# Chunk attention and a gated MLP on one core: value product made transposed, row sums by matmuls with ones, single loads of q and k, and every engine in the order of an event model

## The chip, the cores and the metric

The kernel runs on one core of a Trainium2 chip. The metric is the device time of one execution in microseconds (us), lower is better. The engines are named as the profile names them: PE is TensorE (matmuls), PEld its weight loads, DVE VectorE, ACT ScalarE, POOL GpSimd, SP SyncE, which here only issues DMA transfers (SPq is its queue). The span in a profile is one execution from its first to its last instruction. Some runs fell in a slower state (two of six of e7, one each of e10 and e13, and a few of the kernel before); the ratios leave them out, the medians do not.

## The reference

Eight batches, eight heads, 576 positions, 64 values per head; attention only inside chunks of 64 positions. Its output, as rows of 512 values, goes through a gated MLP whose gate mixes positions with a 576x576 matrix.

```python
scores = scale * np.matmul(q_c, k_c.transpose(0, 1, 2, 4, 3))   # 64x64 per chunk and head
attn = np.exp(scores - max); attn = attn / (sum(attn) + 1e-09)
x = np.matmul(attn, v_c)                                        # -> (8, 576, 512)
h = np.maximum(x @ w_in, 0.0)                                   # 512 -> 1024
u, v = h[..., :512], h[..., 512:]
v_n = (v - mean(v)) / sqrt(var(v) + 1e-06)
v_s = np.einsum('ts,bsd->btd', w_spatial, v_n) + b_spatial[None, :, None]
out = (u * v_s) @ w_out
```

The tokens are worked on as 36 tiles of 128 rows. Every fifth tile of nine lies across two batches.

## The kernel before

Per tile: load q, k and v; cast to bf16 on GpSimd; transpose q and k on TensorE (TR); scores (QK); exponential on ScalarE; value product (AV); normalise on VectorE; transpose the result x (XT), since the input products want x with its features on partitions. Then the input products HV (per tile) and U (per four tiles), the statistics, the spatial products SP (64 units of five matmuls) and the output products FIN (36). Only TensorE and GpSimd are put in a hand-made order here; the others follow it.

```python
def load(t):                                   # two transfers for each of q and k, in halves of four heads
    for name, src in (("q", q), ("k", k)):
        for r0, n, b, s in pieces(t):
            for e in (0, 1):
                nc.sync.dma_start(out=f[r0:r0 + n, e, :],
                    in_=src[b, 4 * e:4 * e + 4, s:s + n, :].rearrange("h (p r) d -> p h (r d)", r=4))
    ...
def AV(t):                                     # out: chunk rows on partitions; column 64 is the row sum
    for h in range(H):
        for c in (0, 1):
            c0 = c * 64
            nc.tensor.matmul(o[c0:c0 + 64, h, 0:65], eT[c0:c0 + 64, h // 4, (h % 4) * 64:(h % 4) * 64 + 64],
                             va[c0:c0 + 64, h, :], start=True, stop=True)
    nc.vector.reciprocal(rz, o[:, :, 64:65])
    nc.vector.tensor_tensor(x, o[:, :, 0:64], rz.to_broadcast([128, H, D]), op=ALU.mult)
def XT(t):
    for m in range(4):
        nc.tensor.transpose(ps[:, m * 128:(m + 1) * 128], x[:, 2 * m:2 * m + 2, :]..., permb)
    nc.vector.tensor_copy(xT[g][:, :, r * 128:(r + 1) * 128], ps[:, 0:512]...)
...
def try_sp():                                  # spatial products of batch b
    ...                                        # only when its statistics group (an odd batch: two) and its input products U are done
    ready = clock[0] + 12.0
```

The softmax here doesn't subtract the row's maximum and nothing guards it: scores larger than these inputs give would overflow.

Of the kernel before, what the change touches and what calls it, by code (L numbers as in the profile page):

```python
# [12 lines left out]
PSUM = bass.MemoryType.PSUM  # L13


@with_exitstack
def kernel(
# [11 lines left out]
    nc = tc.nc  # L29

    B, H, S, D = q.shape
    CH = 64
# [3 lines left out]
    NTOK = B * S  # L36
    NT = NTOK // 128
    NG = NTOK // 512
    HS = S // 2
    att_scale = 1.0 / float(D) ** 0.5  # L40
    out_flat = out.rearrange("b s d -> (b s) d")

    def pool(name, bufs, **kw):
        return ctx.enter_context(tc.tile_pool(name=name, bufs=bufs, **kw))

    consts = pool("consts", 1)
    persist = pool("persist", 1)
    xT_pool = pool("xT_pool", 4)
    uT_pool = pool("uT_pool", 6)
    att_in = pool("att_in", 4)  # L50
    att_bf = pool("att_bf", 4)
    att_sb = pool("att_sb", 3)
    relu_pool = pool("relu_pool", 12)
    vn_pool = pool("vn_pool", 20)
    tail_pool = pool("tail_pool", 3)
    stat_pool = pool("stat_pool", 3)
    bst_pool = pool("bst_pool", 4)
    gat_pool = pool("gat_pool", 3)
    osb_pool = pool("osb_pool", 4)

    ps_tr = pool("ps_tr", 1, space=PSUM)
    ps_sc = pool("ps_sc", 1, space=PSUM)
    ps_o = pool("ps_o", 1, space=PSUM)
    ps_big = pool("ps_big", 3, space=PSUM)

# [4 lines left out]

# [3 lines left out]

    permb = consts.tile([128, 128], BF16, name="permb")
    for c in (0, 1):
        nc.vector.tensor_copy(permb[:, c * 64:c * 64 + 64].rearrange("p (l r) -> p l r", r=4),
                              identb[:, c * 64:c * 64 + 64].rearrange("p (r l) -> p l r", r=4))
# [3 lines left out]
    NVB = 6  # L82
    vaug = [persist.tile([128, H, 65], BF16, name=f"vaug{i}") for i in range(NVB)]
    for i in range(NVB):
        nc.vector.memset(vaug[i][:, :, 64:65], 1.0)

    xT, uT = {}, {}


    w_in_sb = persist.tile([128, 4, d_ff], BF16, name="w_in_sb")  # L90
    w_out_sb = persist.tile([128, 4, d_model], BF16, name="w_out_sb")
    ws_nat = persist.tile([128, 5, S], BF16, name="ws_nat")

    ws_full = [[persist.tile([128, S], BF16, name=f"wsf{p}_{i}") for i in range(4)]
               for p in (0, 1)]
    ws_tail = [persist.tile([128, S], BF16, name=f"wst{p}") for p in (0, 1)]

    w_in_v = moe_w_in.rearrange("(c p) f -> p c f", p=128)

    def load_w_in(part, c0, c1):  # L100
        cols = slice(F, 2 * F) if part == "v" else slice(0, F)
        nc.gpsimd.dma_start(out=w_in_sb[:, c0:c1, cols], in_=w_in_v[:, c0:c1, cols])
# [8 lines left out]
    def load_w_out():  # L111
        nc.gpsimd.dma_start(out=w_out_sb, in_=moe_w_out.rearrange("(c p) f -> p c f", p=128))

    def ws_transpose(p, i):

        if i < 4:
            s0, n, dst = i * 128 + 64 * p, 128, ws_full[p][i]
        else:
            s0, n, dst = (512 if p == 0 else 0), 64, ws_tail[p]
        ps = ps_big.tile([128, 1024], BF16, name="big")  # L120
        for tb in range(5):
            m = 128 if tb < 4 else 64
            nc.tensor.transpose(ps[:n, tb * 128:tb * 128 + m],  # L123
                                ws_nat[:m, tb, s0:s0 + n], identb[:m, :m])
        if (i + p) % 2:
            nc.vector.tensor_copy(dst[:n, :], ps[:n, 0:S])
        else:
            nc.scalar.copy(dst[:n, :], ps[:n, 0:S])


    st = {}

    def pieces(t):

        b, s = divmod(t * 128, S)
        if s + 128 <= S:
            return [(0, 128, b, s)]
        return [(0, 64, b, s), (64, 64, b + 1, 0)]

    def load(t):  # L140
        f32 = {}

        for name, src in (("q", q), ("k", k)):
            f = att_in.tile([128, 2, 4 * D], FP32, name=f"{name}f")
            for r0, n, b, s in pieces(t):
                for e in (0, 1):
                    nc.sync.dma_start(  # L147
                        out=f[r0:r0 + n, e, :],
                        in_=src[b, 4 * e:4 * e + 4, s:s + n, :].rearrange("h (p r) d -> p h (r d)", r=4))
            f32[name] = f  # L150
        f = att_in.tile([128, H, D], FP32, name="vf")
        for r0, n, b, s in pieces(t):
            nc.sync.dma_start(out=f[r0:r0 + n], in_=v[b, :, s:s + n, :].rearrange("h s d -> s h d"))
        f32["v"] = f
        st[t] = {"f32": f32}

    def cast(t, after_each=()):
        f32 = st[t].pop("f32")

        qb = att_bf.tile([128, 4, 2, D], BF16, name="qb")  # L160
        kb = att_bf.tile([128, 4, 2, D], BF16, name="kb")
        for dst, name in ((qb, "q"), (kb, "k"), (vaug[t % NVB][:, :, 0:64], "v")):
            x = f32[name]
            nc.gpsimd.tensor_copy(dst, x if name == "v" else x.rearrange("p e (r d) -> p r e d", r=4))  # L164
            for f in after_each:
                f(name)
        st[t] = {"q": qb, "k": kb}

    def cols(c, m):

        return m * 32 + c * 16

    def TR(t):
        ps = ps_tr.tile([128, 1024], BF16, name="tr")
        for i, name in enumerate(("q", "k")):
            for r in range(4):
                c = i * 512 + r * 128
                nc.tensor.transpose(ps[:, c:c + 128],  # L178
                                    st[t][name][:, r].rearrange("p e d -> p (e d)"), permq)
        qT = att_sb.tile([128, 4, 128], BF16, name="qT")  # L180
        nc.vector.tensor_copy(qT.rearrange("p r c -> p (r c)"), ps[:, 0:512])  # L181
        kT = att_sb.tile([128, 128, 4], BF16, name="kT")
        nc.scalar.copy(kT, ps[:, 512:1024].rearrange("p (r c) -> p c r", r=4))  # L183
        st[t]["qkT"] = (qT, kT)

    def QK(t):
        qT, kT = st[t].pop("qkT")
        sc = ps_sc.tile([128, 2, 512], FP32, name="sc")
        for m in range(4):
            for c, e in ((0, 0), (1, 1), (1, 0), (0, 1)):  # L190
                p0, c0 = e * 64, c * 64
                col = cols(c, m)

                nc.tensor.matmul(sc[c0:c0 + 64, e, m * 64:m * 64 + 64],  # L194
                                 kT[p0:p0 + 64, col:col + 16, :].rearrange("p l r -> p (l r)"),
                                 qT[p0:p0 + 64, :, col:col + 16], start=True, stop=True)
        eT = att_sb.tile([128, 2, 256], BF16, name="eT")
        nc.scalar.activation(eT, sc[:, :, 0:256], AF.Exp, scale=att_scale)  # L198
        st[t]["eT"] = eT

    def AV(t):
        eT = st[t].pop("eT")
        va = vaug[t % NVB]
        o = ps_o.tile([128, H, 128], FP32, name="o")
        for h in range(H):
            for c in (0, 1):
# [320 lines left out]
```

## Time and profile before

The median of the first three runs was 226.71 us (225.56 to 228.22).

| | before |
|---|---|
| profiled span | 226.9 us, in a run timed at 228.2 us |
| PE busy | 194.7 us (86%) |
| DVE, ACT, POOL busy | 123.5, 109.5, 101.5 us |
| first spatial product | 80 us |

The busy time of PE is an upper figure, since matmuls overlap at their ends. TensorE's instructions are cut into units (a tile's transposes, its scores, one group of four matmuls, and so on). The time from one unit's start to the next one's start, at its shortest for this pair of kinds, is called **work**; all that a gap is longer than that is **idle**, a wait or a lowered clock alike, and so is the time up to the first matmul (4.7 us). Before: 183.4 us of work, 39.3 us idle, and about 4 us after the last matmul make the span of 226.9. The count has an error: in the traces of e1 to e8 and e13 to e17 the records of some 30 of the matmuls are missing, which makes a shortest step too short. e14 comes out at 182.1 where before, with the same work, has 183.4. So work can be up to 1.3 us too small there, and idle time too large by as much.

### The profile page before, as it was taken

Reading aid. Unit: us, or ns where it says so; the run is one execution under the profiler, and the core shown is the slowest. Engines: PE = TensorE matmul, PEld = TensorE weight load, DVE = VectorE, ACT = ScalarE, POOL = GpSimd, SP = SyncE. Lnnn points to the kernel's source line nnn. Section 1 sums busy time; section 2 is a strip of 40 time slices with the busy share of each in tenths; the row PEclk is TensorE's granted clock in tenths of the full one; section 3 lists DMA queues with packets and bytes.
Section 4 is the critical chain, followed back from the end, with each engine's and each line's share of the span. In section 5 each row is a group of like instructions: output and inputs, shape, how many; then the busy total and the mean of one; then the engine's idle time right before and its main releaser. Section 6 shows DMA issues by size and latency. Waiting matters only on the chain.

```text
span 226.9 us, 6144 instructions
## 1 busy us (share of the span) xinstructions
PE 194.7 (86%) x2402; PEld 120.7 (53%) x2402; DVE 123.5 (54%) x339; ACT 109.5 (48%) x202; POOL 101.5 (45%) x166
## 2 busy tenths in 40 slices
PE   1236486996795999999979999999999999999993
PEld 0123333754463586567557655576665555656551
DVE  1030533748647775578555766696565487535240
ACT  2221332774575534773544566734537774252523
POOL 3526461657935865278443192895304107040000
PEclk9999857999999999999999999999999999999999
DMA  4999999979557897955989896488822000132223
GB/s 130 188 241 221 212 198 244 242 199 243 154 155 192 226 241 215 275 167 150 235 258 293 240 304 178 123 228 223 305 92 93 2 3 1 56 150 106 107 87 147
DMA packets 65981, 40.40 MB, mean 178 GB/s; under 512 B 40800, under 2 KB 61344, under 8 KB 65952
## 3 DMA queue, kind: packets, MB, share of 16 engines
q1 hardware_dynamic: 63680, 37.76, 58.8%
q0 software_dynamic: 2272, 2.24, 6.8%
q8 instruction: 19, 0.31, 0.6%
q14 instruction: 10, 0.08, 0.1%
HBM read 32.79 MB, written 9.44 MB: 186 GB/s over the span
## 4 chain that ended last, share of the span: by engine, by line
PE 77%; DMA 9%; SPq 6%; ACT 3%; DVE 2%; issue 1%; POOL 0%; ACTq 0%; POOLq 0%
PE big L314 17%; PE big L330 14%; PE big L241 14%; PE big L296 13%; PE tr L178 7%; SPq L147 5%; DMA vf<-in_v_dram 4%; PE tr L221 4%; PE o L208 3%; PE sc L194 3%; DMA kf<-in_k_dram 3%; PE big L123 2%; DMA out_dram<-o_sb 2%; ACT v_relu L244 2%; ACT kT L183 1%
## 5 line engine op out<-in xcount | busy, mean ns | idle before, releaser
L290 POOL TENSOR_SCALAR vn<-v_relu,rstd,nmu 128x512 bf16<-128x512 f32 x32 | 25.0, 790 | 48.4 <-DVE nmu L270 48.4
L321 DVE TENSOR_TENSOR gat<-big,uT 128x288 bf16<-128x288 f32 (+8 forms) x96 | 30.8, 353 | 20.7 <-PE big L314 19.0
L314 PE MATMUL big<-wsf,vn 128*128 128x288 bf16 x256 | 40.4, 285 | 1.5 <-ACT o_sb L333 1.5
L183 ACT COPY kT<-tr 128x512 bf16<-128x512 bf16 x36 | 21.0, 584 | 41.1 <-DVE qT L181 41.1
L241 PE MATMUL big<-w_in_sb,xT 128*128 128x512 bf16 x144 | 38.9, 408 | 0.0
L296 PE MATMUL big<-xT,w_in_sb 128*128 128x512 bf16 x144 | 34.8, 380 | 0.0
L330 PE MATMUL big<-w_out_sb,gat 128*128 128x512 bf16 (+1 forms) x160 | 34.6, 381 | 0.0
L164 POOL CAST kb<-kf 128x512 bf16<-128x512 f32 x36 | 22.1, 613 | 25.5 <-DMA kf<-in_k_dram 23.1
L181 DVE COPY qT<-tr 128x512 bf16<-128x512 bf16 x36 | 15.1, 418 | 33.5 <-PE tr L178 33.4
L247 DVE BATCH_NORM_STATS2 bst<-v_relu 128x6 f32<-128x512 f32 x36 | 24.7, 687 | 15.3 <-ACT v_relu L244 15.2
L333 ACT COPY o_sb<-big 128x512 f32<-128x512 f32 x36 | 21.0, 585 | 24.2 <-PE big L330 20.6
L244 ACT ACTIVATE v_relu<-big 128x512 f32<-128x512 f32 x36 | 21.5, 597 | 23.0 <-PE big L241 21.3
L314 PEld LDWEIGHTS <-vn 128*128 128x128 bf16 x256 | 24.0, 97 | 9.3 <-issue 1.5
L164 POOL CAST qb<-qf 128x512 bf16<-128x512 f32 x36 | 22.0, 612 | 14.5 <-DMA qf<-in_q_dram 8.3
L164 POOL CAST vaug<-vf 128x512 bf16<-128x512 f32 x36 | 22.2, 617 | 13.4 <-DMA vf<-in_v_dram 13.4
L198 ACT ACTIVATE eT<-sc 128x512 bf16<-128x512 f32 x36 | 21.5, 597 | 11.8 <-PE sc L194 11.8
L300 ACT ACTIVATE uT<-big 128x512 bf16<-128x512 f32 x36 | 21.3, 599 | 10.9 <-PE big L296 10.8
L214 DVE TENSOR_TENSOR x<-o,rz 128x512 bf16<-128x512 f32 x36 | 24.9, 692 | 1.0
L226 DVE COPY xT<-tr 128x512 bf16<-128x512 bf16 x36 | 15.1, 418 | 15.8 <-PE tr L221 15.7
L221 PE MATMUL tr<-permb,x 128*128 128x128 bf16 x144 | 14.4, 224 | 10.4 <-ACT kT L183 6.6
L178 PE MATMUL tr<-permq,qb 128*128 128x128 bf16 x144 | 14.9, 230 | 8.8 <-POOL qb L164 7.7
L330 PEld LDWEIGHTS <-gat 128*128 128x128 bf16 (+1 forms) x160 | 13.1, 100 | 14.8 <-issue 1.6
(45 smaller groups left out, 199.3 us busy)
## 6 DMA issues: line engine op xcount, KB each, us to landing
out_dram<-o_sb SPq DMA_DIRECT2D x36, 256.0 KB, 2.9
qf<-in_q_dram SPq DMA_DIRECT2D x64, 128.0 KB, 3.4
kf<-in_k_dram SPq DMA_DIRECT2D x64, 128.0 KB, 3.3
vf<-in_v_dram SPq DMA_DIRECT2D x32, 256.0 KB, 4.2
qf<-in_q_dram SPq DMA_DIRECT2D x16, 64.0 KB, 2.8
kf<-in_k_dram SPq DMA_DIRECT2D x16, 64.0 KB, 2.2
vf<-in_v_dram SPq DMA_DIRECT2D x8, 128.0 KB, 4.1
ws_nat<-in_moe_w_spatial_dram POOLq DMA_DIRECT2D x1, 576.0 KB, 7.5
```

Of the source, the lines that this page charges most:

```text
L164: nc.gpsimd.tensor_copy(dst, x if name == "v" else x.rearrange("p e (r d) -> p r e d", r=4))
L178: nc.tensor.transpose(ps[:, c:c + 128], st[t][name][:, r].rearrange("p e d -> p (e d)"), permq)
L214: nc.vector.tensor_tensor(x, o[:, :, 0:64], rz.to_broadcast([128, H, D]), op=ALU.mult)
L221: nc.tensor.transpose(ps[:, m * 128:(m + 1) * 128], x[:, 2 * m:2 * m + 2, :].rearrange("p h d -> p (h d)"), permb)
L241: nc.tensor.matmul(hv, xT[g][:, cb, r * 128:(r + 1) * 128], w_in_sb[:, cb, F:], start=(cb == 0), stop=(cb == 3))
L244: nc.scalar.activation(vr, hv, AF.Relu)
L247: nc.vector.bn_stats(bst, vr)
L290: nc.gpsimd.tensor_scalar(y, vr, sc, bi, op0=ALU.mult, op1=ALU.add)
L296: nc.tensor.matmul(hu, w_in_sb[:, cb, fb * 128:(fb + 1) * 128], xT[g][:, cb, :], start=(cb == 0), stop=(cb == 3))
L314: nc.tensor.matmul(vs[:, 0:HS], lhsT, rhs, start=(i == 0), stop=(i == 4))
L321: nc.vector.tensor_tensor(gat[b][:, db, half * HS + done:half * HS + done + n], vs[:, done:done + n], uT[g][:, db, r:r + n], op=ALU.mult)
L330: nc.tensor.matmul(po[r0:r0 + n, :], gat[b][:, jb, s:s + n], w_out_sb[:, jb, :], start=(jb == 0), stop=(jb == 3))
```

## The change

Its intent: TensorE is the bound, so give it less to do (no transposes of x), and let it start the heavy stages earlier (an order from a model of all engines, with smaller statistics groups and no fixed delay of 12 us). Four parts go together: (a) the value product gives its result already transposed; the row sums then lie along columns, so they are made for all 64 feature rows at once by matmuls with ones; (b) the reciprocal becomes exp(-ln(sum)) on ScalarE; (c) one transfer each for q and k; (d) a `plan()` that simulates all engines with a table of durations, and all five instruction streams written in its order.

```diff
-                for e in (0, 1):
-                    nc.sync.dma_start(
-                        out=f[r0:r0 + n, e, :],
-                        in_=src[b, 4 * e:4 * e + 4, s:s + n, :].rearrange("h (p r) d -> p h (r d)", r=4))
+                nc.sync.dma_start(out=f[r0:r0 + n].rearrange("p e x -> p (e x)"),
+                                  in_=src[b, :, s:s + n, :].rearrange("h (p r) d -> p h (r d)", r=4))
 ...
-        for h in range(H):
-            for c in (0, 1):
-                nc.tensor.matmul(o[c0:c0 + 64, h, 0:65], eT[...], va[c0:c0 + 64, h, :], start=True, stop=True)
-        nc.vector.reciprocal(rz, o[:, :, 64:65])
-        nc.vector.tensor_tensor(x, o[:, :, 0:64], rz.to_broadcast([128, H, D]), op=ALU.mult)
-    def XT(t): ... 4 transposes, 1 copy
+        for m in range(4):
+            for c, e in ((0, 0), (1, 1), (1, 0), (0, 1)):
+                nc.tensor.matmul(o[e0:e0 + 64, c, m * 64:m * 64 + 64], vb[c0:c0 + 64, 2 * m + e, :],
+                                 eT[c0:c0 + 64, (e * 4 + m) * 64:(e * 4 + m) * 64 + 64], start=True, stop=True)
+        for c, e in ((0, 0), (1, 1), (1, 0), (0, 1)):
+            nc.tensor.matmul(o[e0:e0 + 64, c, 256:512], ones[c0:c0 + 64, :],
+                             eT[c0:c0 + 64, e * 256:e * 256 + 256], start=True, stop=True)
+        nc.scalar.activation(lz, o[:, :, 256:512], AF.Ln)
+        nc.scalar.activation(rz, lz, AF.Exp, scale=-1.0)
+        nc.vector.tensor_tensor(xT[...], o[:, :, 0:256]..., rz..., op=ALU.mult)
 ...
-            return (2 * k0, j, 5) if j < 5 else (2 * k0 + 1, j - 5, 4)      # statistics groups of 5 and 4 tiles
+        out += [(k0, k0 + 1, k0 + 2), (k0 + 3, k0 + 4), (k0 + 5, k0 + 6), (k0 + 7, k0 + 8)]
 ...
-    with tc.manual_schedule(engines={PE, Pool}): ...
+    with tc.manual_schedule(engines={PE, Pool, Activation, DVE, SP}):
+        for o in plan():                        # 36 tiles' operations, durations, buffers, priorities
+            emit[...]
```

## The prediction

> **What bounds the kernel now.** I read the page first, then the chain that ended last, then the groups by shape, then stretches of the timeline. The page, parts 1 and 2:
>
> ```profile
> PE 194.7 (86%) x2402; PEld 120.7 (53%) x2402; DVE 123.5 (54%) x339; ACT 109.5 (48%) x202; POOL 101.5 (45%) x166
> ...
> PE   1236486996795999999979999999999999999993
> ...
> PEclk9999857999999999999999999999999999999999
> DMA  4999999979557897955989896488822000132223
> ```
>
> TensorE (PE) is the bound, but in two regimes. In the first ten slices (57 us) the DMA engines are full and PE is thin (and in slices 5 to 7 at a lowered clock); from about slice 14 (80 us) PE is full to the end. The chain in the second regime:
>
> ```profile
> 131.50 0.45 PE tr L178 x8
> 131.95 1.73 PE big L296 x8
> 134.15 0.25 PE o L208 x16
> 134.40 1.83 PE big L296 x8
> 136.24 0.45 PE tr L178 x8
> ...
> 220.27 2.68 PE big L330 x12
> 223.02 0.58 ACT o_sb L333
> ```
>
> One attention tile per 4.74 us (131.50 to 136.24), PE on the path all the time, and 3.9 us after the last matmul's end (copy, store, landing). How long an operation really occupies PE is read from start to start, since matmuls overlap. One stretch of the timeline:
>
> ```profile
> 106.31 0.39 PE L221 MATMUL tr<-permb,x 128*128 128x128 bf16 x4
> 106.62 0.32 PE L194 MATMUL sc<-qT,kT 64*64 64x64 bf16 x16
> 106.77 0.42 PE L208 MATMUL o<-vaug,eT 64*64 64x65 bf16 x16
> 107.12 2.02 PE L330 MATMUL big<-w_out_sb,gat 128*64 128x512 bf16 x12
> 108.98 0.39 PE L178 MATMUL tr<-permq,qb 128*128 128x128 bf16 x4
> 109.21 0.39 PE L178 MATMUL tr<-permq,kb 128*128 128x128 bf16 x4
> 109.43 0.65 PE L314 MATMUL big<-wsf,vn 128*128 128x288 bf16 x4
> 109.92 0.29 PE L314 MATMUL big<-wst,tail_o 65*128 65x288 bf16 x1
> 110.05 0.65 PE L314 MATMUL big<-wsf,vn 128*128 128x288 bf16 x4
> ```
>
> Start to start: transposes of x 0.31 us, scores 0.15, value product 0.35, transposes of q and k 0.45, one spatial unit (five matmuls) 0.62. A group of four 512-column matmuls takes 0.87 (1.73/2 in the chain), an output tile whose rows cross a batch 0.99 (1.86 - 0.87). PE work of the whole kernel at full clock: attention 36 x (0.45+0.31+0.15+0.35 = 1.26) = 45.4; the two input products 72 x 0.87 = 62.6; spatial 64 x 0.62 = 39.5; output 32 x 0.87 + 4 x 0.99 = 31.8; ten groups of weight transposes, estimated at 0.4 each, 4. Sum 183. The span is 226.9, so 44 us are lost on PE. Where? The first spatial product starts at 80.22 us in the chain. The program puts before it 16 q/k transposes, 13 x transposes, 15 scores, 14 value products, 12+11 input products and the weight transposes: 7.2+4.0+2.3+4.9+20.0+4 = 42 us of work. So 38 of the 44 us are lost before 80 us, about 2 between 80 and 223, 3.9 at the end.
>
> **What the Trainium skill says.** "TensorE: Matmul & The Clock Gate" (Wait — 56ns, not 53.3ns?) gives 215.7 ns from start to start for warm 512-column matmuls; 1.73/8 = 216 ns here, so the second regime has no slack inside its matmuls. "TensorEngine Tiling (Array Packing)" (Key Properties) says that different tiles run in parallel and that a change of mode drains the engine. The trace agrees: sixteen 64x64 scores, spread over four quarters, take 0.15 us, sixteen value products on only two quarters 0.35. "ScalarE: Activation LUTs" (What ACT_TABLE_LOAD costs) has 186 ns + 0.833 ns per column and 93 ns of overlap, and puts Ln and Exp in one table set; 186 + 427 = 613 ns against 597 measured for the exponential, and the trace has a single table load. "TensorE" (What's actually happening) ties the clock to recent activity; the lowered slices 5 to 7 agree.
>
> **The change, part by part.**
>
> Removed: 144 x transposes (0.31 x 36 = 11.2 us of PE), their copies (36 x 418 ns = 15.1 us of VectorE, DVE), the reciprocals (7.2 us), two fills of tail rows per tail tile on GpSimd (4.2 us). The product that normalises stays on DVE (692 ns before) and now writes xT directly.
>
> Value product: still 16 matmuls, now on four quarters like the scores, so about 0.13 us, plus four matmuls with ones of 256 columns, one on each quarter. In parallel they take half of a 512-column matmul, 0.11 us. To this I add an estimated 0.10 to 0.15 us per tile for a further change of mode, as scores and value product no longer stand next to each other. New attention per tile 0.45 + 0.15 + 0.13 + 0.11 + 0.25 (drains) = about 1.09 against 1.26: 0.17 x 36 = 6 us less. New PE total 177.
>
> ScalarE (ACT): a Ln and an Exp of 128x512 per tile, 72 x 0.597 = 43 us more; 16 statistics groups instead of 8 (about 0.5 us each), 4 more; 6 of the 36 output copies move to DVE, 3.5 less. 109.5 + 43.5 = about 153 us, about 148 with overlap. DVE: 123.5 - 15.1 - 7.2 + 6 x 0.6 + a little for the statistics = about 106. Neither exceeds 177, but ACT goes from 48% to some 73%.
>
> Loads: q and k once each per tile instead of twice. An issue takes 0.60 us of the queue in the chain, so 1.8 instead of 3.0 us per tile. The bytes and the rows of 1 KB (q, k) and 256 B (v) stay, and the engines were already full from 5.7 to 57 us (mean share 0.99). Worth 1 or 2 us at the start.
>
> Order: this is the large part. In the changed program the first spatial product comes after only 8 q/k transposes, 7 scores, 7 value products, 6+4 input products and the weight transposes (3.6 + 7 x 0.64 + 8.7 + 4 = 21 us of work). Smaller statistics groups (2 or 3 tiles instead of 4 or 5) and no fixed 12 us delay make that possible. It must wait for tile 7, which comes off a full DMA. In the trace of before:
>
> ```profile
> 42.57 0.40 PE L178 MATMUL tr<-permq,qb 128*128 128x128 bf16 x4
> ```
>
> That is tile 7's. I take 42 us for it in the new kernel. From there PE has spatial and output work to fill every step. Loss before the first spatial product: 42 - 21 = 21 us instead of 38. From there 177 - 21 = 156 us of work.
>
> Sum: 42 + 156 + 3.9 = 202, plus stalls. Before, the saturated regime lost 2 us; with ACT half again as busy, in strict order, and two spatial products that hold a PSUM buffer until the next group's input product, I allow 2 to 4. Predicted 204 us. Seen as a difference from 226.7: 17 from the order, 6 from attention, about 1 given back.
>
> **The rivals.**
> First, the start is bound by DMA, so reordering cannot help and only attention's 6 us come: 220. For it: DMA full to 57 us. Against it: after 57 us DMA is no longer full, yet PE was thin until 80, and with tile 11 landed (its value cast is at 57.6) the work that twelve tiles and their one finished pair of batches allow, about 12 x (1.26 + 2 x 0.87) + 16 x 0.62 + 4 = 50 us, was about half done; I think this one fails.
> Second, ACT becomes the bound: the longer chain per tile (copy, exponential, Ln, Exp, then DVE) in fixed order, with one score and one value buffer, makes PE wait. At 148 us busy it needs 4.1 us per tile against PE's 4.9; bursts of four input products plus attention exceed that for a while. If it costs 0.3 us per tile: 214.
> Third, the ones matmuls run one after another: 3 x 0.11 x 36 = 12 us more: 215.
> Fourth, the modelled order is wrong by a few tenths in places and every engine, now in fixed order, waits for the others: 210 to 225. For it: it includes guessed DMA times, and a store stuck behind waiting loads already cost PE 1.53 us at 119.05. Against it: the times in its table are close to the trace's (0.87 for four matmuls, 0.42 and 0.52 for the q and k copies against 0.418 and 0.584).
> On the good side: an earlier tile 7 and cheap drains would give 195.
>
> **Range and chances.** 204, with 195 to 214 for eight cases in ten: the low end is cheap drains and faster loads, the high end one rival of 10 us. To miss 2% (222) two rivals must hold at once. Faster 0.95, same 0.04, slower 0.01.
>
> **What would show it.** Right: first spatial product between 38 and 46 us; PE full from then on; value product and sums together 0.25 to 0.4 us from start to start; ACT near 150 us busy, DVE near 106; last matmul followed by about 4 us. Wrong: PE dots in its slices after 60 us with waits on lz, rz, xT or on evictions; ones matmuls at 0.11 us apart; a first spatial product later than 50 us.

## The result

The kernel after took 218.54 us (median of five runs, 217.48 to 218.96), beside 227.05 us for the kernel before on the same chip (five runs, 225.56 to 229.76). The ratio is 0.9623, with a 95% interval of 0.9574 to 0.9672. A ratio here and below is the mean time of one kernel's fast runs over the mean of the other's in the same rounds, so it is not quite the ratio of the medians quoted. The kernel became 3.8% faster, where 10% had been predicted: the direction was right, and the time lies outside the range of 195 to 214.

The page of the kernel after, the parts that answer to those shown of before:

```profile
PE 190.8 (88%) x2402; PEld 107.5 (50%) x2402; DVE 109.8 (51%) x280; ACT 146.4 (68%) x284; POOL 96.2 (45%) x158
...
PE   1464689979899999799999999999999989998992
...
PEclk9998558999999999999999999999999999999999
DMA  5999999959389999677599378876840200311224
```

TensorE is now well filled from slice 6 (27 us) instead of slice 14, though before had nines in slices 8, 9 and 12 too; yet its busy time is only 4 us less, and small losses show as 8s and 9s up to the end. The clock is still lowered, now in slices 4 to 7. The new ScalarE work, from the groups (idle before the instruction and its releaser at the right):

```profile
L441 DVE TENSOR_TENSOR xT<-o,rz 128x512 bf16<-128x512 f32 x36 | 24.7, 687 | 17.8 <-ACT rz L434 17.8
...
L431 ACT ACTIVATE lz<-o 128x512 f32<-128x512 f32 x36 | 21.5, 596 | 4.7 <-PE o L427 4.6
...
L434 ACT ACTIVATE rz<-lz 128x512 f32<-128x512 f32 x36 | 22.8, 634 | 0.5
```

Ln and Exp cost 44.3 us of ScalarE together, as foreseen, and ScalarE as a whole is at 146.4 us.

The same accounting as above for both kernels, and for two experiments that come later:

| | first spatial product at | TensorE work | idle before it | idle after it | visits to the 64-wide mode | span |
|---|---|---|---|---|---|---|
| before | 80.1 us | 183.4 | 36.9 | 2.4 | 37 | 226.9 |
| after | 46.8 us | 179.8 | 25.2 | 6.7 | 58 | 215.7 |
| new product and single loads, old order | 72.8 us | 174.6 | 32.5 | 7.1 | 37 | 218.2 |
| all three, scores and value product together, one operation moved | 47.9 us | 175.8 | 27.9 | 6.6 | 38 | 214.5 |

A visit is a row of 64x64 matmuls between others of the full 128 rows; how one is priced follows below. The first spatial product came 33 us earlier, as intended. In TensorE's timeline of before and then of after:

```profile
80.06 0.65 PE L314 MATMUL big<-wsf,vn 128*128 128x288 bf16 x4
```

```profile
46.75 0.65 PE L523 MATMUL big<-wsf,vn 128*128 128x288 bf16 x4
```

But idle time fell by only 7.4 us (39.3 to 31.9) and work by 3.6 us. Where before had lost its time explains this: counted in stretches of 10 us, 29.4 of its 36.9 us had been lost in the first 40 us, only 7.5 us between 40 and 80. After 40 us TensorE had input products and attention to do; that its spatial products came at 80 us only meant that other work came first. Moving them forward reorders work in that stretch, and can win at most those 7.5 us there. After has lost 22.7 us by 30 us, where before had lost 24.5.

Why the first 30 us did not shrink is seen in the chain of work that ended last, here its part from 24 us (start, duration, engine, tile; "issue" steps left out):

```profile
24.06 0.42 DVE qT L394
24.49 0.61 DVE bst L462
...
25.12 0.19 DVE mv L467
...
25.34 0.31 ACT lnv L473
...
25.67 0.20 ACT rstd L474
25.87 0.49 ACT eT L413
...
26.41 0.43 PE o L423 x13
26.84 0.24 PE o L427 x4
...
27.09 0.61 ACT lz L431
...
27.72 0.64 ACT rz L434
...
28.39 0.70 DVE xT L441
...
29.13 1.89 PE big L450 x4
```

Between 24.06 and 29.13 us this is one dependent line of copies, exponentials, sums, Ln, Exp and the multiplication, with TensorE on it for 0.7 us. It passes through one score buffer and one value buffer, and in strict order: the statistics of a finished group (bst, mv, lnv, rstd) stand before the exponential eT that TensorE waits for.

### The profile page after: what moved, and what is told of

It is laid out like the page before. It is cut to its first block, busy times and chain, and to the rows that moved or that the text cites. A ratio compares the mean times of both kernels' runs of the same rounds, so it can differ in the third digit from the quotient of the medians.

```text
span 215.7 us, 6041 instructions
## 1 busy us (share of the span) xinstructions
PE 190.8 (88%) x2402; PEld 107.5 (50%) x2402; DVE 109.8 (51%) x280; ACT 146.4 (68%) x284; POOL 96.2 (45%) x158
## 4 chain that ended last, share of the span: by engine, by line
PE 74%; ACT 10%; DVE 6%; DMA 6%; issue 1%; SPq 1%; POOL 0%; ACTq 0%
PE big L450 15%; PE big L523 15%; PE big L508 15%; PE big L537 15%; PE tr L391 6%; DMA w_in_sb<-in_moe_w_in_dram 3%; PE sc L406 3%; PE o L423 3%; DVE xT L441 2%; ACT rz L434 2%; ACT lz L431 2%; DMA vf<-in_v_dram 2%; ACT kT L397 2%; ACT relu L454 2%; PE big L559 2%; PE o L427 1%
## 5 line engine op out<-in xcount | busy, mean ns | idle before, releaser
L462 DVE BATCH_NORM_STATS2 bst<-relu 128x6 f32<-128x512 f32 x36 | 24.9, 693 | 43.0 <-ACT relu L454 43.0
L491 POOL TENSOR_SCALAR vn<-relu,rstd,nmu 128x512 bf16<-128x512 f32 x32 | 24.8, 785 | 37.9 <-DVE nmu L480 36.0
L381 POOL CAST vb<-vf 128x512 bf16<-128x512 f32 x36 | 22.0, 612 | 43.0 <-PE o L423 21.9
L508 PE MATMUL big<-xT,w_in_sb 128*128 128x512 bf16 x144 | 34.9, 390 | 0.5 <-ACT uT L514 0.3
L537 PE MATMUL big<-w_out_sb,gat 128*128 128x512 bf16 (+1 forms) x160 | 34.9, 381 | 0.0
L441 DVE TENSOR_TENSOR xT<-o,rz 128x512 bf16<-128x512 f32 x36 | 24.7, 687 | 17.8 <-ACT rz L434 17.8
L454 ACT ACTIVATE relu<-big 128x512 f32<-128x512 f32 x36 | 21.5, 598 | 17.0 <-PE big L450 17.0
L383 POOL CAST qb<-qf 128x512 bf16<-128x512 f32 x36 | 22.1, 614 | 20.1 <-issue 15.7
L544 ACT COPY osb<-big 128x512 f32<-128x512 f32 x30 | 17.6, 585 | 14.5 <-PE big L537 14.2
L523 PEld LDWEIGHTS <-vn 128*128 128x128 bf16 x256 | 23.4, 97 | 7.8 <-POOL vn L491 0.3
L431 ACT ACTIVATE lz<-o 128x512 f32<-128x512 f32 x36 | 21.5, 596 | 4.7 <-PE o L427 4.6
L383 POOL CAST kb<-kf 128x512 bf16<-128x512 f32 x36 | 22.1, 613 | 3.3 <-DMA kf<-in_k_dram 3.2
L450 PEld LDWEIGHTS <-xT 128*128 128x128 bf16 x144 | 13.3, 101 | 20.2 <-DVE xT L441 5.1
L434 ACT ACTIVATE rz<-lz 128x512 f32<-128x512 f32 x36 | 22.8, 634 | 0.5
L508 PEld LDWEIGHTS <-w_in_sb 128*128 128x128 bf16 x144 | 13.6, 100 | 16.2 <-issue 2.2
```

Of the source, the lines that this page charges most:

```text
L383: nc.gpsimd.tensor_copy(new(x + "b", (x + "b", t), [128, 4, 2, D], BF16), f.rearrange("p e (r d) -> p r e d", r=4))
L431: nc.scalar.activation(new("lz", ("lz", t), [128, 2, 256], FP32), T["o", t][:, :, 256:512], AF.Ln)
L434: nc.scalar.activation(new("rz", ("rz", t), [128, 2, 256], FP32), T.pop(("lz", t)), AF.Exp, scale=-1.0)
L441: nc.vector.tensor_tensor(T["xT", g][:, :, r * 128:r * 128 + 128].rearrange("p m (c s) -> p c m s", c=2), o[:, :, 0:256].rearrange("p c (m ...
L450: nc.tensor.matmul(hv, T["xT", g][:, cb, r * 128:(r + 1) * 128], w_in_sb[:, cb, F:], start=(cb == 0), stop=(cb == 3))
L454: nc.scalar.activation(new("relu", ("relu", t), [128, F], FP32), T.pop(("hv", t)), AF.Relu)
```

## The experiments

My theory after the result, on record with e1 and e2: the new order only moves the spatial products forward and hardly fills idle time, so the gain is the product's; what is missing was lost in drains, in the lowered clock and in stalls of the strict order. The rivals: the gain came from the order; the start is bound by the transfers' bytes; the ScalarE chain holds TensorE up; the model's order is off against the machine. The texts on record state what each of those at issue expects of a run. Differences between two ratios are given in per cent of the time before.

The rival of a model that is off could be looked at without a run: `plan()` in the kernel gives a start time for every operation, and these were set against the trace. At 21 us the trace is 1.1 us late; by the plan's 31 us it is 5.0 us late, after a stretch in which the clock record stands at 0.5 (20.2 to 33.8 us); then the lag stays or shrinks, to 2.4 us at the end. Most of the idle time is in the plan itself: with its own durations it has 22.1 us before its first spatial product, at 42.10 us, and 8.4 us after it (measured: 25.2 and 6.7). What the machine adds is the lag, 4.65 us at the first spatial product.

### Taking the change apart, first group

**e1_old_product_new_order**: the new order and single loads, with the old value product, the reciprocal on VectorE and the transposes of x put into the model with their durations.

```diff
-        op(("LZ", t), "ACT", 0.52, ...); op(("RZ", t), "ACT", 0.52, ...)
+        op(("RZ", t), "DVE", 0.86, ...)        # reciprocal and multiplication
+        op(("XP", t), "PE", 0.23, ...)         # transposes of x
```

> The order without the new product: x transposes, reciprocal of 8 columns and vaug as before, merged loads and an event-model order made anew for these operations (with one guard more: a spatial product waits until the input product it will be multiplied with has been issued; without it the plan gets stuck). Theory A (mine: the new order only moves the spatial products forward and hardly fills idle TensorE time): TensorE work 183 us plus about 30 more changes of array mode of 0.2 us = 189, idle as after or more (32 to 36), tail 4: 223 to 231 us, no faster than before. Rival B (the order is where the gain came from): 217 to 221 us.

**e2_new_product_old_order**: the kernel before with the new value product (parts a and b) alone. Two transfers each of q and k stay, now of every second head.

> The new product, sums with ones and Ln/Exp in the order of before (two loads each, ScalarE and VectorE ordered by the scheduler as before). Scores and value product stay neighbours here, so the array changes mode 37 times and not 58. Theory A: TensorE work 183.4 - 7 = 176 us, idle as before (37 to 41), so 217 to 220 us, as fast as the whole change or nearly. Rival B (order is the gain): 222 to 226 us. Rival C (72 more ScalarE instructions become the bound without a new order): above 226 us.

**e3_two_loads**: the kernel after with two transfers each of q and k.

> The changed kernel with q and k again loaded by two transfers each (heads of even and odd number), nothing else. Theory A (the DMA engines are full at the start and the number of issues does not matter): within 1 us of the changed kernel. Rival: 72 more issues of 0.6 us on the queue delay the first tiles and the stores: 2 to 5 us slower.

**e4_dve_reciprocal**: the kernel after with the reciprocal of the 128x512 sums on VectorE.

```diff
-        nc.scalar.activation(lz, T["o", t][:, :, 256:512], AF.Ln)
-        nc.scalar.activation(rz, lz, AF.Exp, scale=-1.0)
+        nc.vector.reciprocal(rz, T["o", t][:, :, 256:512])
```

> The changed kernel with one VectorE reciprocal of 128x512 in place of Ln and Exp on ScalarE, and the order planned anew for it (0.66 us assumed). If the reciprocal takes about 0.7 us: ScalarE falls from 146 to about 104 us busy, VectorE rises from 110 to about 135. Theory A1 (the ScalarE chain causes the TensorE stalls of 6.7 us after the first spatial product and part of the slow start): 3 to 6 us faster than the changed kernel. Rival (ScalarE has slack and is not to blame): within 1.5 us. If the reciprocal is slow (over 1.5 us): slower by 5 us or more.

Measured, beside 228.81 us for before:

| run | median us | ratio to before (95%) | work | idle before / after the first spatial product | visits |
|---|---|---|---|---|---|
| e1_old_product_new_order | 240.62 | 1.0554 (1.0475 to 1.0633) | 189.5 | 25.8 / 20.3 | 68 |
| e2_new_product_old_order | 229.55 | 1.0087 (1.0009 to 1.0164) | 174.6 | 41.3 / 6.8 | 37 |
| e3_two_loads | 222.43 | 0.9771 (0.9696 to 0.9846) | 179.4 | 25.8 / 11.6 | 58 |
| e4_dve_reciprocal | 308.99 | 1.3548 (1.3456 to 1.3641) | 180.6 | 39.4 / 82.9 | 64 |

No part carries the gain alone, and my theory missed both e1 (223 to 231 us expected) and e2 (217 to 220 us). The order with the old product is slower than before. By e1's own plan the last matmul ends at 229.1 us, against 209.3 in the plan of the kernel after, so e1 tests what this model makes of the old product, not every possible order. The product alone takes some 8 us of work from TensorE and gives all of it back as idle time. e3 is slower than the kernel after by 2.8 us (against e5 of the next group), inside the 2 to 5 us that the rival expected, not within 1 us as theory A had it. e4 shows that the 128x512 reciprocal is no substitute for Ln and Exp (its order was planned for 0.66 us). Its group of reciprocals, by shape:

```profile
L430 DVE RECIPROCAL rz<-o 128x512 f32<-128x512 f32 x36 | 120.8, 3354 | 20.4 <-PE o L426 20.2
```

3354 ns against 596 + 634 on ScalarE: every tile's chain grows by 2 us, VectorE gets 121 us more to do, and TensorE waits for it.

How a visit to the 64-wide mode is priced: first, in TensorE's timeline of the kernel after, a stretch in which scores stand alone (start, duration, engine, line, what).

```profile
103.90 0.65 PE L523 MATMUL big<-wsf,vn 128*128 128x288 bf16 x4
104.39 0.29 PE L523 MATMUL big<-wst,tail_e 65*128 65x288 bf16 x1
104.61 0.32 PE L406 MATMUL sc<-qT,kT 64*64 64x64 bf16 x16
104.86 0.23 PE L391 MATMUL tr<-permq,qb 128*128 128x128 bf16 x1
```

Then, in the same timeline, a stretch in which value product, sums and scores are neighbours.

```profile
111.92 0.32 PE L423 MATMUL o<-eT,vb 64*64 64x64 bf16 x16
112.07 0.28 PE L427 MATMUL o<-eT,ones 64*64 64x256 bf16 x4
112.18 0.29 PE L406 MATMUL sc<-qT,kT 64*64 64x64 bf16 x16
112.41 0.39 PE L537 MATMUL big<-w_out_sb,gat 128*128 128x512 bf16 x1
```

From start to start, a spatial unit of five matmuls takes 0.62 us in a row of such units, but 0.71 when scores follow (103.90 to 104.61). The scores take 0.25 (104.61 to 104.86), but only 0.15 before another 64-wide unit. Over all occurrences, the entry costs 0.093 us and the exit 0.103, so 0.195 per visit. Within a visit, the value product takes 0.15 us and the four matmuls with ones 0.11 (111.92, 112.07, 112.18). Attention after is 0.446 + 0.148 + 0.148 + 0.112 = 0.854 per tile, plus 58 visits of 0.195: 42.1 us in all, against 45.4 before. The order itself makes 21 visits more than before (58 against 37), 4.1 us.

### Order, clock and bytes, second group

**e5_after_again**: the kernel after, unchanged, so that the others have it on the same chip.

> The changed kernel itself, as the yardstick of this group of runs: ratio 0.962 to before again (217 to 220 us).

**e6_neighbours**: from tile 6 on, the scores of tile t and the value product of tile t-1 are one operation of the model, and a change of mode costs more in it.

```diff
+            op(("QA", t), "PE", 0.41, t - 1.0, [("EQ", t), ("EK", t), ("EX", t - 1), ("Cv", t - 1)], ...)
-SWITCH = 0.06
+SWITCH = 0.1
```

> The changed kernel, but from tile 6 on the scores of a tile and the value product and sums of the tile before are one unit on TensorE, so that the array changes its mode 38 times and not 58; the plan counts 0.1 us per change. Theory A (each visit to the 64-wide mode costs 0.195 us beside its matmuls, and that is what ate the gain of the product): TensorE work 180 down to 176, 2.5 to 4.5 us faster than the changed kernel. Rival (drains lie beside other waits, or the tied pair now waits for its slower half): within 1 us of it.

**e7_warm**: about 150 small matmuls into an unused part of the score buffer, between the first five tiles' units, which keep TensorE active. The result is not touched.

```diff
+    WARM = {("TR", 0): 12, ("QK", 0): 5, ("TR", 1): 8, ("QK", 1): 5, ("HV", 0): 6, ("TR", 2): 2, ("QK", 2): 5,
+            ("AV", 2): 12, ("HV", 2): 4, ("TR", 3): 8, ("QK", 3): 5, ("TR", 4): 6}
+        for i in range(2 * WARM.get(name, 0)):
+            nc.tensor.matmul(scp[:, i % 2, 64:128], permq, identb[:, 0:64], start=True, stop=True)
```

> The changed kernel with some 150 small matmuls on constants into unused PSUM columns, put after the early products (tiles 0 to 4), where TensorE waited anyway. They keep it active. Theory H (the granted clock of a half from 20 to 34 us is why the machine fell some 5 us behind the plan there): the clock stays at 1.0 and the first spatial product comes 3 to 5 us earlier, time 3 to 5 us less. Rival (arrival of data and the chain of copies set the start, since runs with a mean clock of 1.0 were no faster): within 1.5 us.

**e8_no_q**: q is not loaded, k is cast in its place. A third of the attention's input bytes is gone, the compute is the same. Its output is wrong, which doesn't matter for the time. (The comparison with the reference still passed: with inputs this small the scores are near zero, and the weights nearly equal.)

> Wrong result on purpose: q is never loaded, both casts read k, so a third of the input bytes is gone; order unchanged. Theory D (the first 40 us are bound by the DMA engines): the first spatial product moves from 46.8 us to 41 or less and the time falls by 5 us or more. Rival L (they are bound by the length of the chain per tile and the fixed order, data being there): first spatial product within 3 us, time down by at most 3 us.

Measured, beside 227.33 us for before:

| run | median us | ratio to before (95%) | work | idle before / after the first spatial product | visits |
|---|---|---|---|---|---|
| e5_after_again | 219.20 | 0.9647 (0.9605 to 0.9689) | 179.4 | 25.6 / 7.1 | 58 |
| e6_neighbours | 221.98 | 0.9757 (0.9708 to 0.9807) | 175.9 | 26.0 / 14.6 | 38 |
| e7_warm | 216.26 | 0.9495 (0.9446 to 0.9544) | 179.4 | 23.4 / 7.1 | 58 |
| e8_no_q | 218.04 | 0.9588 (0.9530 to 0.9645) | 179.4 | 23.8 / 7.1 | 58 |

e8: with a third fewer input bytes, 0.6% is gained, within the two intervals, and the first spatial product comes at 45.4 us (47.2 in e5), not at the 41 that theory D expected. In this order the bytes are not what bounds the start.

e7 gains 1.5%, 3.5 us; the first spatial product comes at 45.0 us, 2.1 earlier than in e5 where theory H expected 3 to 5. The plan is the same, and between 23 and 34 us e7's lag behind it stays at 2.0 to 3.2 us, where the kernel after's grew from 1.1 to 5.0: what was lost there goes with the lowered clock. The k transposes of one tile in TensorE's timeline of e7, in a stretch of the start:

```profile
24.12 0.39 PE L393 MATMUL tr<-permq,kb 128*128 128x128 bf16 x4
```

And in that of e5, the kernel after:

```profile
24.55 0.63 PE L391 MATMUL tr<-permq,kb 128*128 128x128 bf16 x4
```

0.39 instead of 0.63 us for four transposes. This also shows a trap: for e5 the mean granted clock is given as 1.0, since its clock record begins only at 33.2 us. The durations tell that its TensorE was slow before that.

e6 took the 20 visits away, and 3.5 us of work with them, as the price of a visit says; but it lost more to a new stall. VectorE's timeline of e6 in this stretch:

```profile
45.83 7.01 DVE L508 TENSOR_SCALAR tail_o<-relu,rstd,nmu 64x512 bf16<-64x512 f32 x1
52.87 0.69 DVE L447 TENSOR_TENSOR xT<-o,rz 128x512 bf16<-128x512 f32 x1
```

GpSimd's timeline of e6, the first and the last of a row of casts:

```profile
46.38 0.60 POOL L389 CAST qb<-qf 128x512 bf16<-128x512 f32 x1
...
51.95 0.60 POOL L389 CAST kb<-kf 128x512 bf16<-128x512 f32 x1
```

TensorE's timeline of e6, with the idle time before the instruction in brackets:

```profile
53.62 0.61 PE L456 MATMUL big<-w_in_sb,xT 128*128 128x512 bf16 x1 [5.62 <-DVE xT L447]
```

One VectorE instruction on half a tile took 7.01 us, where the same takes 0.55 us elsewhere (0.55 is the shortest and the usual one of its four occurrences). It lies beside eleven back-to-back casts on GpSimd (46.38 to 52.55) and ends when the row ends. The xT that stands behind it on VectorE started at 52.87 us, and TensorE waited 5.62 us; the clock was lowered from 48.9 to 59.2 us. In e1 the same instruction took 4.80 us once and in e4 4.67, each time too beside a row of casts and ending 0.3 us after the last of them; beside a single cast (138.4 us in the kernel after) it took 0.59.

### Is it that instruction? Third group

**e9_neighbours_tail_act**: e6 with that one operation on ScalarE, in the kernel and in the model, whose order is made anew.

```diff
-        nc.vector.tensor_scalar(to[0:64], relu[64:128], sc[64:128], bi[64:128], op0=ALU.mult, op1=ALU.add)
+        nc.scalar.activation(to[0:64], relu[64:128], AF.Identity, scale=sc[64:128], bias=bi[64:128])
```

> The kernel with scores and value product as neighbours (38 visits to the 64-wide mode), with the odd tail rows (four instructions of 64x512) normalised on ScalarE and not on VectorE, because one of them took 7.0 us on VectorE beside GpSimd's casts there. Theory A (mode changes cost 0.195 us each, and only that one starved instruction hid the gain): no instruction over 2 us on VectorE, TensorE work 176 us, 215 to 217.5 us, ratio about 0.948 to 0.957. Rival (tying the pair makes TensorE wait as much as it saves): ratio 0.962 to 0.970, with the idle time after the first spatial product at 10 us or more.

**e10_best**: e9, neighbours only from tile 10 on and at a higher priority, with the small matmuls of e7.

> The same with the pair tied from tile 10 on and at a slightly higher priority, and with the small matmuls that keep TensorE's clock up. If both effects are separate they add: 3 us from the clock and 3 to 4 from the modes, 211 to 214 us, ratio 0.93 to 0.942. Rival (the two gains are the same idle time): ratio 0.945 or more.

**e11_no_exp**: the kernel after without the Exp that follows Ln (xT is multiplied by the logarithm; three buffers for it instead of two), so ScalarE has 23 us less work and the chain per tile one link less. Its output is wrong, which doesn't matter for the time.

> Wrong result on purpose: the changed kernel without the Exp of the logarithm (36 ScalarE instructions of 0.63 us less on the chain of each tile), same order. Theory S (ScalarE's load and the longer chain cause the TensorE idle time): the 7 us after the first spatial product fall below 4 and the start gets 1 to 3 us shorter; time 3 to 6 us less, ratio 0.94 to 0.952. Rival (idle time is built into the fixed order): ratio 0.957 or more.

**e12_old_order_no_exp**: e2 without that Exp. Its output is wrong, which doesn't matter for the time.

> Wrong result on purpose: the new product in the order of before, again without that Exp. There the new product saved 8.8 us of TensorE work and idle time grew by as much. Theory S (the chain through ScalarE is what takes it back): idle time falls by 4 us or more, 222 to 225 us, ratio 0.97 to 0.985. Rival (the order of before itself, which issues fixed amounts of fill between steps, takes it back): ratio 0.995 or more.

Measured, beside 228.40 us for before:

| run | median us | ratio to before (95%) | work | idle before / after the first spatial product | visits |
|---|---|---|---|---|---|
| e9_neighbours_tail_act | 215.77 | 0.9477 (0.9431 to 0.9522) | 175.8 | 27.9 / 6.6 | 38 |
| e10_best | 213.61 | 0.9382 (0.9321 to 0.9443) | 176.5 | 26.9 / 6.1 | 41 |
| e11_no_exp | 215.74 | 0.9494 (0.9440 to 0.9548) | 179.8 | 23.8 / 5.5 | 58 |
| e12_old_order_no_exp | 229.33 | 1.0075 (1.0032 to 1.0118) | 175.7 | 36.8 / 11.0 | 37 |

e9 answers the question: on ScalarE each of the four operations takes 0.81 us, the stall is gone, and the fewer visits show in the time: 0.9477 against 0.9647 for the kernel after of the group before, 1.7%. e10 beats both kernels, by 6.2% before and by some 2.7% after (from the ratios of two groups, as for e9 and e11), and its results are correct.

e11 gives 1.5% over after, in time what theory S expected: the ScalarE chain has a share in the idle time (1.8 us of it before the first spatial product, 1.6 after). But 5.5 us stay after the first spatial product where S expected less than 4, so it is not the whole cause. e12 was to show the weight of ScalarE in the old order and is inconclusive: its idle time before the first spatial product did fall, from 41.3 to 36.8 us, but at 156 us TensorE waited 6.6 us for an output copy that waited 7.44 us for a store which stood behind waiting loads in the one queue. The two effects cancel, so the run does not measure the Exp there.

### What the product lacked, fourth group

e2's missing gain was still open. Its first 60 us had moved fewer bytes than those of before. The suspect is the queue that issues the transfers.

**e13_product_and_loads**: e2 with single loads, so parts (a), (b) and (c) in the old order.

```diff
-                for e in (0, 1):
-                    nc.sync.dma_start(out=f[r0:r0 + n, e, :], in_=src[b, e::2, s:s + n, :]...)
+                nc.sync.dma_start(out=f[r0:r0 + n].rearrange("p e x -> p (e x)"), in_=src[b, :, s:s + n, :]...)
```

> Product and single loads in the order of before. If the single loads are worth what they are in the changed kernel (about 1.2%): ratio 0.99 to 1.0, and the order is then worth the remaining 3%. If the queue of transfers was what took the product's gain back in the order of before: ratio 0.965 to 0.98.

**e14_loads_alone**: the kernel before with single loads.

> The kernel before with single loads of q and k and nothing else. Theory A (DMA engines full at the start, queue not the bound later): ratio 0.99 to 1.0. Rival (issue time on the queue delays tiles): 0.975 to 0.985.

**e15_order_loads_tail_act**: e1 with the stalling operation on ScalarE.

> New order and single loads with the old product, without the starved instruction (4.8 us in e1). If that was the only fault of e1: ratio 0.99 to 1.02 and idle time after the first spatial product about 8 us. If the order made by this event model is bad for the old product in itself (its chain is longer on TensorE and VectorE and 68 visits to the 64-wide mode): ratio 1.03 to 1.05, idle time after the first spatial product over 12 us.

Measured, beside 227.90 us for before:

| run | median us | ratio to before (95%) | work | idle before / after the first spatial product | visits |
|---|---|---|---|---|---|
| e13_product_and_loads | 220.92 | 0.9680 (0.9567 to 0.9792) | 174.6 | 32.5 / 7.1 | 37 |
| e14_loads_alone | 226.69 | 0.9935 (0.9862 to 1.0007) | 182.1 | 34.7 / 3.9 | 37 |
| e15_order_loads_tail_act | 233.62 | 1.0235 (1.0162 to 1.0308) | 189.3 | 24.9 / 13.8 | 68 |

One run of e13, at 228.3 us, was slow and is left out of the ratio, which rests on three runs. e13 lies where the rival of the queue had it, e14 where theory A had it. e15 falls between its two expectations: the stalling operation was worth 3.2% of e1's 5.5% loss, and the rest stays, as its own plan has it (last matmul at 227.6 us).

The first 60 us of e2 in one row (busy time and count of PE, PEld, DVE, ACT, POOL; then clock, the transfers' share, GB/s):

```profile
0.00:60.00 60.00, 32.03 (x461) 18.37 (x466) 16.16 (x38) 27.53 (x50) 26.86 (x48) 0.88 0.90 205
```

The largest wait of TensorE among e2's waits (us in total, times, longest):

```profile
PE tr L174 <- POOL qb L160: 14.2, 5, 4.8
```

The same row of e13:

```profile
0.00:60.00 60.00, 37.09 (x576) 21.55 (x585) 20.44 (x48) 35.49 (x65) 34.38 (x61) 0.97 1.04 243
```

And the same wait in e13:

```profile
PE tr L173 <- POOL qb L159: 9.1, 4, 4.6
```

In e2 the 72 issues of the first 60 us kept the transfers at 205 GB/s; with 56 issues they reached 243, and TensorE's waits for q fell from 14.2 to 9.1 us. The waits of the issuing queue itself in e2:

```profile
SPq L143 <- POOL vaug L160: 3.8, 12, 0.6
...
SPq L143 <- POOL kb L160: 1.4, 3, 0.5
```

And in e13:

```profile
SPq L142 <- POOL kb L159: 34.6, 20, 6.9
```

The queue of e13 waits 34.6 us for casts to free the input buffers, over the whole run, so it runs ahead of the compute; in e2 no such wait exceeds 3.8 us in total, so the queue was behind. Both queues are busy with issues, the short gaps between them included, for 56 and 57 of the first 62 us; what single loads change is how much each issue moves. Of the 72 issues of e2 59 take 0.65 us or less; of the 56 of e13 only 34 do, the others up to 3.6 us, with the transfers' share at 1.04. That points to the issues as e2's limit and to the transfers as e13's, without proving it. So in the old order with the new product the loading of q and k in halves held the start back. Two things are not separated here: the issues' own time and the smaller transfers, and in e2 and e3 the halves are of every second head, where before has four adjacent ones. That may have to do with e2's loads being even later than those of before (the v cast of tile 11 started at 62.7 us, 57.6 before, 54.8 in e13).

### Settling what the order is worth, fifth group

**e16_product_and_loads_again** (e13 unchanged) and **e17_after_third** (the kernel after), five rounds each, on one chip.

> Product and single loads in the order of before once more. If the order is worth nothing: the same ratio as the changed kernel in this group within 0.005. If the order is worth 1% or more: ratio higher than the changed kernel's by 0.01 or more.

> The changed kernel as the partner of the run before: 0.962 to 0.967.

Beside 227.84 us for before, e16 took 220.63 us, ratio 0.9674 (0.9630 to 0.9717), and e17 218.75 us, ratio 0.9597 (0.9556 to 0.9637). The difference, 0.8% (the medians differ by 1.9 us, the profiled runs by 2.7, and every run of e17 is faster than every run of e16), is what the order gives once product and loads are there. It lies between the two expectations, 0.5% and 1%; e17 itself came out a little below the 0.962 expected.

All the combinations, as ratios to before:

| | old order | new order |
|---|---|---|
| old product, two loads | 1 | not run |
| old product, single loads | 0.9935 | 1.0554 (1.0235 with the stalling operation moved) |
| new product, two loads | 1.0087 | 0.9771 |
| new product, single loads | 0.9680, 0.9674 | 0.9623, 0.9647, 0.9597 |

The parts do not add. Product and single loads alone do next to nothing, and together give 3.2%. With them, the order takes 6.7 us more idle time away and pays 4.1 us for it in work, the 21 more visits to the 64-wide mode (e16 and e17 with the work of the complete traces, 175.7 and 179.8). So what the order is worth depends on what is there already: 0.8% with product and single loads, but 3.2% with the product and loads in halves (e2 against e3). Loads in halves are worth avoiding by 4.1% in the old order and 1.2% in the new one.

## Why the prediction was right or wrong

**The sum.** It was 42 us to the first spatial product, 156 us of work from there, 3.9 us at the end and 2 us of stalls. Measured: 46.75, 158.3, 4.0 and 6.7, which is 215.7, the span. The miss of 11.8 us is 4.7 + 2.3 + 0.1 + 4.7. A further 1.8 us comes from setting a sum over the span equal to the time: the profiled run of 215.7 us was timed at 217.48.

**"17 from the order": this step failed.** The loss before the first spatial product was 25.2 us instead of the 21 worked out, and 4.3 us came back as idle time later, so 7.4 us were gained and not 17. And the order pays for them: against the old order with the same product and loads (e16, e17) it takes away 6.7 us of idle time and adds 4.1 us of work, and the time falls by 1.9 us (2.7 in the profiled runs). What had been predicted of the other parts, 6 and 1 or 2 us, is what product and single loads gave together: 7.2 us (227.84 to 220.63). The fault in the reasoning is to have put the loss "before 80 us" down to the late spatial products. The number 38 was right, but 29.4 of the 36.9 us measured lie in the first 40 us, where a tile's chain and the loads set the pace, and which the new order leaves nearly as they were (22.7 us lost by 30 us, 24.5 before). The bound's idle time per stretch would have told this in the trace of before; its page shows TensorE at nine tenths in slices 8 and 9, 40 to 51 us, in the stretch that the prediction calls thin. The kernel's own `plan()` would have told it too: its last matmul ends at 209.3 us, which with the 3.9 us of the end is 213, not 204.

**"I take 42 us" for tile 7** failed by 4 us. Its transposes started at 46.30 us (42.57 before), although its q and k had been cast by 34.9 us: the arrival of data, which I had read as the limit, was not. The plan has these transposes at 40.84 us and the first spatial product at 42.10, so the 42 agrees with the plan by luck. The machine was 5.5 and 4.65 us behind it, and most of that came up while the clock was lowered. No term of the sum was for that.

**"6 from attention"** was mis-sized: 3.6 us less work. Within a visit everything came as worked out: value product 0.148 (0.13), sums 0.112 (0.11), in parallel, so the third rival falls. The term that was off is the drains: 0.25 per tile had been estimated, 58 visits of 0.195 are 0.31 per tile, and the old attention had held the same cost inside its own 37 visits. At 37 visits the new attention saves 7.7 us of work (183.4 to the 175.7 of e12), more than predicted; it is the order's 21 visits that give 4.1 of them back.

**Loads "1 or 2 us at the start"** was mis-sized. In the new order two loads cost 1.2% (e3 against e5), 2.8 us. In the old order with the new product they cost 4.1% (e2 against e13), so there the single loads are what lets the product's gain through; a part of it may be that e2's halves are of every second head. Alone they give 0.65%, within the noise of that run.

**"I allow 2 to 4" of stalls** was too little: 6.7 us after the first spatial product.

**Rivals.** The first (bound by bytes) falls with e8, though the number of issues did matter. The second (ScalarE) is right in part: taking one Exp away gives 1.5%, about 3.5 us. The fourth (order off by tenths) is right in part: the machine was 4.65 us behind the plan at the first spatial product and 2.4 at the end, and most of the idle time was planned. e6 shows a larger fault of the model, an instruction that its table of durations does not foresee.

**Right:** ScalarE at 146.4 us (148 predicted), VectorE at 109.8 (106), 4 us after the last matmul, TensorE as the bound with work of 179.8 (177).

What stays open: how much of the lag behind the plan is the clock alone (e7 takes 1.7 of the 4.65 us away, and its small matmuls cost time themselves); which property of the loads in halves holds the start back (number of issues, size, or which heads lie together); how much of the 22.7 us lost in the first 30 us could be had by a second score and value buffer, for which no run was made; and the order with old product and two loads was not run.

## What to carry to other kernels

Find out when the bound engine is idle, stretch by stretch, before you put a price on starting a stage earlier: a stage that starts late costs nothing where the engine had other work. If the order comes from a model, read the model's own end time before you predict. Count the changes of matmul tile size in any new order, for each has a price (0.195 us a visit here, 21 of them against 6.7 us of idle time won), and count the issues of a transfer queue as well as its bytes. When parts of a change relieve limits that hide each other, run the combinations: here two parts that gave -0.9% and +0.65% alone gave 3.2% together.

## What the Trainium skill lacked or had wrong

- "TensorEngine Tiling (Array Packing)", Key Properties, says that a change of mode drains TensorE and gives no price. Here a visit to the 64x64 mode between full-size matmuls cost 0.195 us (0.093 on entry, 0.103 on exit).
- "SBUF — State Buffer", Who interferes with whom, says that a VectorE instruction in a mode with two ports contends with GpSimd: whoever issues first holds the shared ports for its whole instruction, and the other blocks. It mentions a VectorE slowdown of 6.8 times, but not that the loser may stay blocked over a row of instructions: one VectorE `tensor_scalar` of 64x512 took 7.01 us instead of 0.55 beside eleven back-to-back GpSimd casts of 0.56 us each, and moving it to ScalarE took the stall away. That the lock is the cause is inferred from these times, and no run shows which mode the instruction was in.
- "VectorE: DVE Perf Modes", First, the fixed hardware budget, names a repeat count of 8 for the reciprocal and gives no duration. A reciprocal of 128x512 took 3354 ns, 6.55 ns per column, against 1230 ns for Ln and Exp on ScalarE.
- "TensorE: Matmul & The Clock Gate", Seeing it yourself, calls the clock records unreliable. One more form of it: before the first record (33.2 us in one run) nothing is recorded, and the mean clock is then given as 1.0 while four transposes took 0.63 instead of 0.39 us.
- "DMA: Bandwidth & Descriptors", Issuing engines are not separate DMA queues, calls the time to initiate a transfer usually small relative to the transfer. Here the issuing queue was busy with issues for 56 of the first 62 us (e2), and two issues of 128 KB instead of one of 256 KB each for q and k went with 205 instead of 243 GB/s and cost 4.1% (e2 against e13). The runs do not tell the issues' time from the size of the transfers.
